# A mixture-of-experts kernel whose first product adds its three half-precision terms in one set of PSUM columns

## Chip, cores and metric

The kernel runs on one core of one Trainium2 chip. The metric is the device time of one execution in microseconds, the median of several runs; lower is better. One further execution was profiled, and the trace, the views and the rows below are from that one.

## What is computed

Three stages follow each other; each one's output is the next one's input:

```python
# 1. a complex linear recurrence with (4, 8, 768, 48) inputs, its output reshaped to x: (3072, 384)
# 2. a mixture of 8 experts, one per token (the argmax of the gate's logits):
for e in range(E):
    mask = e_idx == e
    h = np.maximum(x[mask] @ w1[e], 0.0)              # 384 -> 1024
    out[mask] = gate_w[mask, None] * (h @ w2[e])      # 1024 -> 384
# 3. one dense two-layer network for all tokens, 384 -> 2048 -> 384
h = x @ w_in
g = h * (1.0 / (1.0 + np.exp(-1.702 * h)))
return g @ w_out
```

The change is in stage 2.

## The kernel before

**Halves.** Every float32 operand of the matmuls in stages 2 and 3 is held as two float16 halves, a high one and the remainder, the low one. A product is the sum of three terms: high by high, high by low (of the weights) and low (of the tokens) by high.

**Blocks and quarters.** The tokens are sorted by expert into 26 blocks of 128 tokens; each block has one expert, whose number is read from memory at run time. The 1024 hidden columns are worked in four quarters `q` of 256 (`FQ`). The loop in `moe` runs over the 4 x 26 = 104 pairs `(q, b)`. The weights' tile `w` holds, for each expert and each of the three slices of 128 inputs, 256 high columns and next to them 256 low ones, so a 512-wide operand covers both halves.

**The work for one pair.** `gemm1(q, b)` makes 128 x 256 of `h` in a PSUM tile `ph` (three buffers). `turn(q, b)` transposes it on the tensor engine (PE) into `pt` (two buffers), and writes the two halves of its positive part: the high one, `hT[:, 0]`, by the scalar engine (ACT, L1092), the low one by the vector engine (DVE, L1093), which waits for the high one. `gemm2(q, b)` makes the second product in `py` with six 384-wide matmuls (L1104), and DVE adds it into `acc` (L1109 in the first quarter, L1111 later). `turn` runs two pairs behind `gemm1` and `gemm2` two more behind that (`LAG`), so for each pair PE's order is: `gemm1(b)`, the transposes of `b - 2`, `gemm2(b - 4)`.

**What runs beside it.** All five engines work through their instructions in the order in which the program text issues them. In the first quarter, `split` also transposes each block's tokens (L1067) and makes their halves (L1068 on ACT, L1069 on DVE), and PE reads the block's expert number into a register (`value_load`, L1074). Every matmul whose weights depend on that number has an address computation ahead of it in PE's queue: the program order prints it as `ISA`, the profile as `FUSED_REGOPS`. During each quarter, `halves` makes the next quarter's weights: ACT scales and rounds them (L996, L998, L1001), GpSimd (POOL, L999) or DVE (L1003) takes the remainders. From the second quarter on, `narrow` turns the 64-bit weights of stage 3 into halves in six steps for each tile, with DVE integer operations (L945 to L949, L960, L966), one ACT rounding (L956) and one DVE remainder (L963). The result is stored from a single buffer to memory by the queue of SyncE (SP, L969, `wh<-w`): ACT's next L956 writes that same buffer, so it waits until the store has landed. `narrow` advances by 6 x 21 / 66 = 1.91 steps per pair, that is one tile every 3.14 pairs.

Of the kernel before, what the change touches and what calls it, by code (L numbers as in the profile page):

```python
# [12 lines left out]
F32 = mybir.dt.float32  # L13
# [4 lines left out]
ALU = mybir.AluOpType  # L18
# [4 lines left out]
P = 128  # L23
# [25 lines left out]
FQ = F // NQ  # L49
KD = DM // P  # L50
# [957 lines left out]
def moe(tc, cst, rt, wp, st, we, yd, lo, hi, x, psum, w0=None, w64=None, wh=None, ffn=None):  # L1008


    nc = tc.nc
    with ExitStack() as c2:
# [20 lines left out]
        xT = x.rearrange("p (b h k n) -> p b h k n", b=nb, h=2, k=KD)  # L1033
# [4 lines left out]
        ph_, pt_, py_, ps_ = psum  # L1038
# [32 lines left out]
        def gemm1(q, b):  # L1071
            w = ws[q]
            if b not in reg:
                reg[b] = nc.tensor.value_load(rt.eid[0:1, b:b + 1], min_val=0, max_val=E - 1)  # L1074
            e = reg[b]
            ph = ph_.tile([P, 2 * FQ], F32, tag="ph", name=f"ph{q}_{b}")
            for k in range(KD):
                o = k * 2 * FQ
                nc.tensor.matmul(ph, lhsT=xT[:, b - lo, 0, k, :], rhs=w[:, e, o:o + 2 * FQ], start=k == 0, stop=False)  # L1079
                nc.tensor.matmul(ph[:, :FQ], lhsT=xT[:, b - lo, 1, k, :], rhs=w[:, e, o:o + FQ], start=False, stop=k == KD - 1)  # L1080
            h = wk.tile([P, FQ], F32, tag="h", name=f"h{q}_{b}", bufs=3)
            nc.scalar.copy(h, ph[:, FQ:])  # L1082
            nc.vector.tensor_tensor(out=h, in0=ph[:, :FQ], in1=h, op=ALU.add)  # L1083
            return h

        def turn(q, b, h):
# [62 lines left out]
        for q, b in seq:  # L1149
# [11 lines left out]
            if q == 0 and b > lo:  # L1161
                split(b + 1)
            hs.append((q, b, gemm1(q, b)))
            if q == 0 and b == lo:
                split(b + 1)
# [27 lines left out]
        while hs:  # L1193
            q, b, h = hs.pop(0)
# [475 lines left out]
```

## Time and profile before

| | |
|---|---|
| median of 3 runs | 969.53 us (969.28 to 970.78) |
| the profiled execution's own time | 970.08 us |
| its span, first to last instruction | 968.3 us |
| stage 2's four quarters, from the first second product | 317.45 to 567.3 us of the span |
| mean granted clock of the tensor engine | 0.972 of full speed |

The 1.8 us between the profiled time and its span lie around the program. In the rows below, PE is the tensor engine's matmuls, PEld its weight loads and PEldq its queue's own work (the last is no busy time). A matmul's row gives its duration in the pipeline, which is longer than its distance to the next one; what a matmul costs is read from the starts. The line numbers in the rows are those of the kernel before; in the changed kernel, lines behind L1079 stand one lower in the text, so that the number is one higher (the transposes of `h` are L1090 there, `gemm2` is L1105).

### The profile page before, as it was taken

What the parts mean: (1) busy time and instruction counts of PE and PEld (TensorE: products, weight loads), DVE (VectorE), ACT (ScalarE), POOL (GpSimd) and SP (SyncE); (2) the same over time, 40 slices, a digit from 0 to 9 for tenths busy, and PEclk for the clock granted to TensorE, in tenths of its full rate; (3) what the DMA queues carried; (4) which work ended last, traced back from release to release, by engine and by line L of the source; (5) the groups of instructions that cost most, each with busy time, mean ns of one, the idle gap of its engine ahead of it and who ended that gap; (6) DMA issues with size and microseconds to landing.
All of it is one profiled execution on the core that took longest, in us unless ns stands there. A gap on an engine that the chain in (4) does not pass through costs nothing.

```text
span 968.3 us, 17226 instructions
## 1 busy us (share of the span) xinstructions
PE 892.4 (92%) x5972; PEld 582.7 (60%) x5972; DVE 631.5 (65%) x1376; ACT 536.8 (55%) x1057; POOL 248.0 (26%) x213
## 2 busy tenths in 40 slices
PE   3899899999976999989999999989999999999994
PEld 2778687888865666655556644435645546456662
DVE  4788888888985898988999669996053171340000
ACT  7879768776553876765763456766063261440000
POOL 1212234112434673542530122233120100001110
PEclk9899999999986999999999999999999999999998
DMA  8530432221352664645647331220110000000000
GB/s 277 204 118 31 149 123 84 76 84 43 138 183 62 213 180 135 211 141 171 189 131 239 123 115 56 93 82 11 48 41 9 25 1 17 17 1 32 26 25 19
DMA packets 40403, 94.98 MB, mean 98 GB/s; under 512 B 6546, under 2 KB 19347, under 8 KB 40307
## 3 DMA queue, kind: packets, MB, share of 16 engines
q1 hardware_dynamic: 35138, 77.87, 24.7%
q0 software_dynamic: 4736, 14.69, 5.0%
q8 instruction: 56, 0.92, 0.4%
q10 hardware_dynamic: 432, 1.18, 0.4%
q14 instruction: 41, 0.33, 0.1%
HBM read 74.84 MB, written 18.81 MB: 97 GB/s over the span
## 4 chain that ended last, share of the span: by engine, by line
PE 44%; DVE 14%; DMA 4%; issue 3%; ACT 2%; POOL 0%; ACTq 0%; POOLq 0%; DVEq 0%; SPq 0%
PE fpo L1308 19%; PE fph L1288 12%; PE py L1104 5%; PE ph L1079 4%; DVE w L960 2%; DMA wh<-w 2%; PE ph L1080 2%; DVE acc L1111 2%; DVE x L1292 2%; DVE h L1083 1%; PE pt L1089 1%; DVE hT L1093 1%; DVE w L966 1%; DVE w L963 1%; PE px L1067 1%
## 5 line engine op out<-in xcount | busy, mean ns | idle before, releaser
L1288 PE MATMUL fph<-fx,fw 128*128 128x512 f16 x864 | 192.2, 379 | 5.7 <-DVE x L1292 4.8
L1292 DVE SCALAR_TENSOR_TENSOR x<-fph,x 128x512 f32<-128x512 f32 x96 | 65.9, 688 | 129.8 <-ACT x L1291 128.4
L1288 PEld LDWEIGHTS <-fw 128*128 128x128 f16 x864 | 84.4, 98 | 104.3 <-issue 8.9
L1308 PE MATMUL fpo<-fw,gT 128*128 128x384 f16 x768 | 125.3, 326 | 0.0
L1104 PE MATMUL py<-w,hT 128*128 x624 | 119.0, 328 | 1.1
L1079 PE MATMUL ph<-w,x 128*128 x312 | 108.9, 383 | 1.1 <-ACT x L1068 0.8
L1312 ACT ACTIVATE x<-fpo,fsm 128x384 f32<-128x384 f32 x24 | 13.9, 581 | 167.5 <-PE fpo L1308 167.5
L1308 PEld LDWEIGHTS <-gT 128*128 128x128 f16 x768 | 75.1, 98 | 49.9
L1291 ACT ACTIVATE x<-fph,fsm 128x512 f32<-128x512 f32 x96 | 65.6, 684 | 49.0 <-PE fph L1288 36.1
L999 POOL TENSOR_TENSOR w<-ws,w 128x768 f16<-128x768 f32 x40 | 68.3, 1708 | 85.2 <-ACT w L998 81.5
L1080 PE MATMUL ph<-w,x 128*128 x312 | 85.7, 275 | 1.8 <-DVE x L1069 1.6
L1313 POOL DMA_INDIRECT out<-x,fto x24 | 23.2, 968 | 245.3 <-ACT x L1312 245.3
L1104 PEld LDWEIGHTS <-hT 128*128 128x128 f16 x624 | 61.2, 98 | 32.5 <-issue 4.0
L1082 ACT COPY h<-ph 128x256 f32<-128x256 f32 x104 | 38.5, 370 | 56.2 <-PE ph L1080 49.1
L1308 PE MATMUL fpo<-fw,x 128*128 128x384 f16 x384 | 62.7, 326 | 0.0
L1083 DVE TENSOR_TENSOR h<-ph,h 128x256 f32<-128x256 f32 x104 | 43.4, 417 | 26.5 <-ACT h L1082 24.1
L517 PE MATMUL pt<-c,f 128*96 128x128 f32 x384 | 53.9, 280 | 4.0 <-DVE u L747 1.9
L1308 PEld LDWEIGHTS <-x 128*128 128x128 f16 x384 | 37.6, 98 | 25.0
L517 PEld LDWEIGHTS pt<-c,f 128*96 128x96 f32 x384 | 43.2, 130 | 14.5 <-issue 6.5
L535 PE MATMUL pt<-zq,zk 96*128 96x128 f32 x384 | 51.4, 283 | 0.0
L1079 PEld LDWEIGHTS <-x 128*128 128x128 f16 x312 | 30.8, 99 | 31.3 <-ACT x L1068 1.6
L535 PEld LDWEIGHTS pt<-zq,zk 96*128 96x128 f32 x384 | 47.5, 196 | 2.0 <-ACT zk L525 0.6
(238 smaller groups left out, 1755.7 us busy)
## 6 DMA issues: line engine op xcount, KB each, us to landing
ws<-in_we SPq DMA_DIRECT2D x61, 384.0 KB
w<-in_w SPq DMA_DIRECT2D x32, 384.0 KB
qk<-in_qk SPq DMA_DIRECT2D x6, 1152.0 KB
yd<-acc SPq DMA_DIRECT2D x26, 192.5 KB
xd<-row SPq DMA_DIRECT2D x6, 589.5 KB
ar<-in_ar SPq DMA_DIRECT2D x6, 576.0 KB
ai<-in_ai SPq DMA_DIRECT2D x6, 576.0 KB
v<-in_v SPq DMA_DIRECT2D x6, 576.0 KB
```

The source lines that it names most:

```text
L517: nc.tensor.transpose(pt[:2 * D, h, :], T[FF][:, k, j * H + 4 * i + h].rearrange("p i d -> p (i d)"), cst["ident"])
L535: nc.tensor.matmul(ps[:, h - 4 * i, :], lhsT=T[ZK][:, h, :], rhs=T[ZQ][:, h, :], start=True, stop=True)
L999: nc.gpsimd.tensor_tensor(out=wv[:, :, 1, :], in0=sv, in1=wv[:, :, 0, :], op=ALU.subtract)
L1079: nc.tensor.matmul(ph, lhsT=xT[:, b - lo, 0, k, :], rhs=w[:, e, o:o + 2 * FQ], start=k == 0, stop=False)
L1080: nc.tensor.matmul(ph[:, :FQ], lhsT=xT[:, b - lo, 1, k, :], rhs=w[:, e, o:o + FQ], start=False, stop=k == KD - 1)
L1082: nc.scalar.copy(h, ph[:, FQ:])
L1083: nc.vector.tensor_tensor(out=h, in0=ph[:, :FQ], in1=h, op=ALU.add)
L1104: nc.tensor.matmul(py, lhsT=hT[:, hl, j, :], rhs=w[:, e, o + off:o + off + DM], start=i == 0, stop=i == n - 1)
L1288: nc.tensor.matmul(ph, lhsT=s.wi[f][:, a, k, :], rhs=xT[b][:, k], start=i == 0, stop=i == 3 * KD - 1)
L1291: nc.scalar.activation(h, ph, AF.Sigmoid, scale=sig)
L1292: nc.vector.scalar_tensor_tensor(out=h, in0=ph, scalar=GS, in1=h, op0=ALU.mult, op1=ALU.mult)
L1308: nc.tensor.matmul(po, lhsT=gT[:, f, a, g * P:(g + 1) * P], rhs=s.wo[f][:, b, :], start=i == 0, stop=i == 3 * s.NF - 1)
```

## The change

`gemm1` no longer makes 512 columns per slice, of which the right 256 hold the high-by-low terms. Each of the three terms of a slice is a 256-wide matmul of its own, and all nine add into the same 256 columns of `ph`. ACT then copies the finished sum to `h`, where before it copied the right half and DVE added the left half to it.

```diff
-            ph = ph_.tile([P, 2 * FQ], F32, tag="ph", name=f"ph{q}_{b}")
+            ph = ph_.tile([P, FQ], F32, tag="ph", name=f"ph{q}_{b}")
+            i = 0
             for k in range(KD):
-                o = k * 2 * FQ
-                nc.tensor.matmul(ph, lhsT=xT[:, b - lo, 0, k, :], rhs=w[:, e, o:o + 2 * FQ], start=k == 0, stop=False)
-                nc.tensor.matmul(ph[:, :FQ], lhsT=xT[:, b - lo, 1, k, :], rhs=w[:, e, o:o + FQ], start=False, stop=k == KD - 1)
+                for hx, hw in ((0, 0), (0, 1), (1, 0)):
+                    o = (2 * k + hw) * FQ
+                    nc.tensor.matmul(ph, lhsT=xT[:, b - lo, hx, k, :], rhs=w[:, e, o:o + FQ], start=i == 0, stop=i == 3 * KD - 1)
+                    i += 1
             h = wk.tile([P, FQ], F32, tag="h", name=f"h{q}_{b}", bufs=3)
-            nc.scalar.copy(h, ph[:, FQ:])
-            nc.vector.tensor_tensor(out=h, in0=ph[:, :FQ], in1=h, op=ALU.add)
+            nc.scalar.copy(h, ph)
             return h
```

PE's queue before, the last of the three slices of block 3 in a later quarter and the transposes that follow (`x` is `xT`, `w` the weights, and the first number in a tile's name is the block):

```order
L1079 LDWEIGHTS x
L1079 ISA
L1079 MATMUL ph_3_5678<-w_4482,x 128x512
L1080 LDWEIGHTS x
L1080 ISA
L1080 MATMUL ph_3_5678<-w_4482,x 128x256
L1089 MATMUL pt_1_5688<-c_60,h_1_5626 128x128 x2
```

The same slice in the changed kernel:

```order
L1081 LDWEIGHTS x
L1081 ISA
L1081 MATMUL ph_3_5736<-w_4488,x 128x256
L1081 LDWEIGHTS x
L1081 ISA
L1081 MATMUL ph_3_5736<-w_4488,x 128x256
L1081 LDWEIGHTS x
L1081 ISA
L1081 MATMUL ph_3_5736<-w_4488,x 128x256
L1090 MATMUL pt_1_5748<-c_60,h_1_5683 128x128 x2
```

Two weight loads, two address computations and two matmuls per slice have become three of each; the transposes follow as before.

DVE's queue before, over two pairs of the second quarter:

```order
L1083 TENSOR_TENSOR h_12_5972<-ph_12_5965,h_12_5972 128x256
L1093 SCALAR_TENSOR_TENSOR hT_10_5978<-pt_10_5975,hT_10_5978 128x256
L1111 SCALAR_TENSOR_TENSOR acc_4366<-py_8_5981,rs_4368,acc_4366 128x384
L966 SCALAR_TENSOR_TENSOR w_3_5897<-w_3_5798,w_3_5897 128x384
L1083 TENSOR_TENSOR h_13_6003<-ph_13_5996,h_13_6003 128x256
L1093 SCALAR_TENSOR_TENSOR hT_11_6009<-pt_11_6006,hT_11_6009 128x256
L1111 SCALAR_TENSOR_TENSOR acc_4366<-py_9_6012,rs_4368,acc_4366 128x384
```

The same engine in the changed kernel, from one pair to the next:

```order
L1094 SCALAR_TENSOR_TENSOR hT_11_6089<-pt_11_6086,hT_11_6089 128x256
L1112 SCALAR_TENSOR_TENSOR acc_4366<-py_9_6092,rs_4368,acc_4366 128x384
L945 TENSOR_SCALAR w_4_6102<-w_4_5967 128x384
L946 TENSOR_SCALAR w_4_6102<-w_4_6102 128x384
L949 TENSOR_SCALAR w_4_6102<-w_4_6102 128x384
L1094 SCALAR_TENSOR_TENSOR hT_12_6126<-pt_12_6123,hT_12_6126 128x256
```

The addition (L1083) that stood ahead of each L1093 is gone, and a pair's work on DVE begins with the low half of `hT`; nothing else changes places.

## Rows read from the trace of the kernel before

**Rows 1.** Engines: busy us (share of the span), instructions; the page's first part.

```profile
PE 892.4 (92%) x5972; PEld 582.7 (60%) x5972; DVE 631.5 (65%) x1376; ACT 536.8 (55%) x1057; POOL 248.0 (26%) x213
```

**Rows 2.** Busy us (instructions) by engine, PEclk, DMA, GB/s; first products' quarters, core 0.

```profile
317.45:383.40 65.95, 64.28 (x426) 43.37 (x425) 59.11 (x147) 48.41 (x143) 34.78 (x45) 1.00 0.57 177
383.40:446.00 62.60, 58.70 (x366) 35.87 (x365) 56.43 (x124) 41.24 (x88) 27.39 (x16) 1.00 0.50 161
446.00:511.50 65.50, 60.58 (x366) 36.33 (x365) 59.43 (x129) 44.14 (x95) 27.75 (x16) 0.97 0.55 170
511.50:567.30 55.80, 55.62 (x357) 35.29 (x356) 42.67 (x102) 22.64 (x63) 4.09 (x5) 1.00 0.51 164
```

**Rows 3.** The page's group: busy us, mean ns, idle before, releaser.

```profile
L1083 DVE TENSOR_TENSOR h<-ph,h 128x256 f32<-128x256 f32 x104 | 43.4, 417 | 26.5 <-ACT h L1082 24.1
```

**Rows 4.** In order of time, 420.7 to 423.05: start us, us, engine, line, operation.

```profile
420.80 0.38 PE L1079 MATMUL ph<-w,x 128*128 x1
...
421.02 0.27 PE L1080 MATMUL ph<-w,x 128*128 x1
421.02 0.10 PEld L1079 LDWEIGHTS <-x 128*128 128x128 f16 x1
...
421.12 0.38 PE L1079 MATMUL ph<-w,x 128*128 x1
...
421.77 0.38 PE L1089 MATMUL pt<-c,h 128*128 128x128 f32 x2
...
422.04 1.14 PE L1104 MATMUL py<-w,hT 128*128 x6
...
423.01 0.38 PE L1079 MATMUL ph<-w,x 128*128 x1
```

**Rows 5.** In order of time, PE, 328.5 to 329.0, first quarter.

```profile
328.58 0.49 PE L1067 MATMUL px<-c,r 128*128 128x128 f32 x3
328.91 0.38 PE L1079 MATMUL ph<-w,x 128*128 x1
```

**Rows 6.** PE's queue, L1104, 430.84 to 431.39: count, min/median/max ns, first and last start.

```profile
L1104 PEldq FUSED_REGOPS  x5: 55/55/55, 430.8 to 431.4; - x5
```

**Rows 7.** PE's queue, L1074, 328.24 to 330.60, same columns.

```profile
L1074 PEldq FUSED_REGOPS  x2: 151/151/151, 328.2 to 330.6; - x2
L1074 PEldq TENSOR_LOAD <-eid x1: 298/298/298, 330.2 to 330.2; - x1
```

**Rows 8.** Who waited for whom, 383.4 to 511.5: us, times, longest us.

```profile
ACT w L956 <- DMA wh<-w: 15.1, 9, 2.9
DVE h L1083 <- ACT h L1082: 11.0, 12, 3.7
```

**Rows 9.** The chain that ended last by line, 383.4 to 511.5.

```profile
by line: DMA wh<-w 15.7%; DVE acc L1111 12.1%; DVE w L960 11.9%; DVE h L1083 8.6%; DVE hT L1093 7.7%; issue 6.3%; DVE w L963 5.9%; PE py L1104 5.5%; DVE w L966 3.7%; PE ph L1079 3.5%; ACT ws L996 3.5%; DMA ws<-in_we 3.0%; ACT w L998 2.9%; A
```

**Rows 10.** The same chain by line, 317.45 to 383.4.

```profile
by line: PE py L1104 35.9%; PE ph L1079 23.7%; PE ph L1080 12.6%; PE px L1067 8.4%; PE pt L1089 7.9%; DVE rs L1056 2.2%; issue 1.7%; DVE x L1069 1.6%; ACT w L1001 1.1%; ACT h L1082 1.0%; DVE acc L1109 0.8%; ACT x L1068 0.7%; DVE h L1083 0.6
```

**Rows 11.** In order of time, 393.0 to 396.8: a copy, its addition, a store.

```profile
393.16 0.35 ACT L1082 COPY h<-ph 128x256 f32<-128x256 f32 x1
...
394.68 0.42 DVE L1083 TENSOR_TENSOR h<-ph,h 128x256 f32<-128x256 f32 x1
...
396.72 0.39 SPq L969 DMA_DIRECT2D wh<-w  x1
```

**Rows 12.** In order of time, 400.9 to 403.0: after that store.

```profile
401.00 0.52 ACT L956 ACTIVATE w<-w 128x384 f16<-128x384 f32 x1 [2.88 <-DMA wh<-w]
...
402.15 0.36 ACT L1082 COPY h<-ph 128x256 f32<-128x256 f32 x1
...
402.41 0.39 ACT L1092 ACTIVATE hT<-pt 128x256 f16<-128x256 f32 x1
402.55 0.42 DVE L1083 TENSOR_TENSOR h<-ph,h 128x256 f32<-128x256 f32 x1 [1.22 <-ACT h L1082]
...
402.89 0.41 DVE L1093 SCALAR_TENSOR_TENSOR hT<-pt,hT 128x256 f16<-128x256 f32 x1
```

## Prediction

> **What bounds the kernel now.** I read the page first: PE is busy for 92% of the span and DVE for 65% [rows 1]. Such averages say little about one stage, so next came the busy time by stretch, cut at the starts of the four quarters [rows 2]. There the reader should see DVE: 56.43 of 62.60 us in the second quarter and 59.43 of 65.50 us in the third, next to a PE that looks busy as well. Third came the order of time, which gives what PE needs when nothing holds it up. Six first-product matmuls take 0.97 us (420.80 to 421.77), two transposes 0.27 us at most and 0.22 us at the pace of a 256-wide matmul, six second-product matmuls 0.97 us (422.04 to 423.01) [rows 4]. That is 2.17 us for a pair (q, b). In the first quarter three more transposes add 0.33 us (328.58 to 328.91) [rows 5]: 2.50 us.
>
> Against these floors the stretches show what is lost. PE runs 60 more instructions in the first stretch than in the second [rows 2], three for each of 20 pairs, so its floor is 20 x 2.50 + 6 x 2.17 = 63.0 of 65.95 us: 2.9 us lost. The second quarter's is 26 x 2.17 = 56.4 of 62.60 (6.2 lost), the third's 56.4 of 65.50 (9.1 lost). The fourth is at its floor for nearly all its length.
>
> Where do those 15.3 us go? In the chain for 383.4 to 511.5, PE's lines are small and DVE's large: L1083, the addition that the change removes, has 8.6% of 128.1 us, 11.0 us [rows 9]. In the first quarter the same line has 0.6%, and PE nearly everything [rows 10]. The waits say how the two engines catch each other: ACT waits 15.1 us in all for the store `wh<-w` to land [rows 8]. One case in order of time: the copy of 393.16 is done at 393.51, but the addition begins only at 394.68, because DVE is behind; the store behind it is issued at 396.72 [rows 11]; ACT, which needs the store's buffer, stands until 401.00 [rows 12], and with it the copies and the halves that PE needs.
>
> **The change, part by part.**
>
> *Columns.* A pair's first product has 3 x (512 + 256) = 2304 columns before and 9 x 256 = 2304 after. The pace of one 512-wide and one 256-wide matmul is 0.32 us (420.80 to 421.12) [rows 4]; three 256-wide ones at the 0.10 to 0.11 us between L1080 and the next L1079 are 0.32 us as well. What is left is a few nanoseconds for each of three more instructions, at most 0.01 us a pair; I take 0.0075 us x 104 = **+0.8 us**.
>
> *Weight loads.* 312 more, 0.10 us each. The load that starts at 421.02 runs under the 256-wide matmul of 421.02, and the next matmul starts on time at 421.12 [rows 4], so 0.10 us of load fits under 256 columns: nothing, with about 0.01 us of cover to spare. The Trainium skill ("TensorE: Matmul & The Clock Gate", "What overlaps and what doesn't") states that a load overlaps a running matmul only where the two use different row groups; these use all rows. By that rule the sum would be about 31 us worse (below), and the rows above speak against it.
>
> *Address computations.* Also 312 more, and here PE's queue has a pace of its own. Five of L1104 start between 430.84 and 431.39, from 430.8 to 431.4 [rows 6]: four distances in 0.50 to 0.55 us, about 0.134 us each. That is faster than the six second-product matmuls they serve (0.97 / 6 = 0.162 us [rows 4]), so it is not the array that sets it, and slower than a 256-wide matmul (0.107 us). The queue runs ahead of the array, so what counts is the sum for a pair. In the first quarter one round, from one L1074 to the next, takes 2.30 to 2.36 us [rows 7] for twelve such matmuls and the reading of the expert's number; it fits under 2.50 us. With three more it is 2.35 + 3 x 0.134 = 2.75 us and no longer fits. Twenty pairs at 2.75 are 55.0 us, where 20 x 2.50 + 2.9 = 52.9 us are spent now: +2.1 if the slower pace swallows all that is lost there today, +5.0 if it swallows nothing. I take **+3.7**, a little above the middle, since the lost time has other causes (DVE's L1056 and L1069 stand in that chain [rows 10]). In the other quarters 15 x 0.134 = 2.01 us stays under 2.17: between 0 and, if the queue needs 0.03 us a pair more than PE, 78 x 0.03 = +2.3; I take **+0.4**, for pairs just after a stall, when the queue has no lead.
>
> *The addition.* 104 x 417 ns = 43.4 us of DVE's busy time go [rows 3]. What it holds up is less, 0.34 us (402.55 to 402.89 [rows 12]), so 11.0 us in the chain are 32 passes. In 12 cases DVE had been waiting for the copy [rows 8]. Then little is won: the next operation, L1093, also needs ACT's L1092, which starts at 402.41 and takes 0.39 us, so it could start at about 402.82 in place of 402.89 [rows 12]: 0.07 us, times 12, 0.8. The other 20 passes give 0.34 each, 6.8. I take **-7.4** of 7.6, since PE's floor is near. Bounds: -1, if every gap closes with another wait; -11.0, the whole of the line in the chain.
>
> *The waits.* The transposes now need ACT's copy, which is earlier than the addition was; their other wait, for the buffer `pt` that L1093 frees two pairs before, stays and is the later of the two. A buffer `ph` comes free after the copy. Nothing else is queued differently. At the drain behind the last pair one addition lies open: **-0.3**.
>
> *Sum.* 0.8 + 3.7 + 0.4 - 7.4 - 0.3 = -2.8: 967.3 us against the profiled execution's 970.08, which is 0.55 above the median; so 966.7 in terms of the median.
>
> **The rivals.**
>
> *The queue wins.* The first quarter pays in full (+5.0), the others 1 to 2, and the gain in the middle shrinks to 2 to 4, because ACT, the store and DVE close into a loop without the addition: store at 396.72, buffer free at 401.00, L1093 at 402.89 [rows 11, 12] is 6.2 us, and with L1111 and L960 behind it easily more than the 3.14 x 2.17 = 6.8 us of a tile. For it: the store's latency is the chain's first entry with 15.7%, L960's 11.9% is larger than the addition's [rows 9]. Against it: 20 of 32 passes were not released by ACT. Sum +2 to +5, 971.5 to 974.5. It decides once the gain in the middle is under 4.9 us. Chance 0.24.
>
> *Both cancel.* Within 0.2%, about what a measurement of this kernel can tell from no change (1.9 us): gain in the middle of 3 to 6.7. Near 969.5. Chance 0.18.
>
> *DVE was the root.* DVE's lag is what makes stores late, so without it most of the 15.3 us go, 11 to 13, and the first quarter pays only 2.1: 960 to 962. For it: DVE has 90% in those quarters [rows 2] and would have about 75%. Against: L960's duration and the store remain. Chance 0.1.
>
> *The queue is no limit.* The address rows last 55 ns each [rows 6]; if only that counted, fifteen take 0.83 us, the terms 3.7 and 0.4 fall away, and the sum is -6.9: 962.6. Against it stands the distance of 0.134 us, which holds a matmul, its load and its address together. The Trainium skill (same page, "Wait — 56ns, not 53.3ns?") gives the queue about 62 ns for each matmul where the sequencer decodes it, and with such a figure too it would be no limit; it says nothing of computed addresses. Chance 0.06.
>
> *The loads don't hide.* 312 x 0.10 = +31, 1000 us; [rows 4] speak against it. Chance 0.02.
>
> **How the numbers follow.** The forecast (a gain over 1.9 us, up to 9) has 0.40, its own range 961.5 to 967.6. Faster is this with the third and the fourth rival, 0.56; same 0.18; slower 0.26. The range 960.5 to 973.5 leaves out the loads, the far end of the first rival and part of the third.
>
> **What would show it.** Right: nine matmuls 0.11 us apart in the second to fourth quarters and a pair at 2.17 to 2.20; a first quarter whose pairs lie about 2.75 us apart with PE's idle time put to no engine; the second and third quarters shorter by some 7 us, with ACT's wait for `wh<-w` well under 15.1. Wrong: a first quarter that keeps 2.50 us (the queue hides it), pairs at 2.25 or more in the fourth quarter (it is dearer than I think), or L956 still waiting 15 us (the loop lives without the addition).

## The result

The changed kernel takes 977.39 us in the median of 5 runs (974.60 to 979.78), the kernel before 969.85 (969.28 to 970.78, 5 runs): a ratio of 1.0084, 95% interval 1.0066 to 1.0101. The change costs about 8 us. The forecast, 966.7, had the sign wrong, and the time lies above the stated range, which ended at 973.5.

The profiled execution took 979.78 us with a span of 977.9, 9.6 more than before. These rows of its page answer to [rows 1] and [rows 3]: the engines, the granted clock in the 40 slices, and the group of the nine first-product matmuls.

```profile
PE 906.2 (93%) x6284; PEld 617.4 (63%) x6284; DVE 605.4 (62%) x1272; ACT 537.8 (55%) x1057; POOL 248.1 (25%) x213
...
PEclk9889999899986999999999999999999999999998
...
L1081 PE MATMUL ph<-w,x 128*128 x936 | 128.0, 273 | 1.8 <-ACT x L1068 0.8
```

DVE is busy for 605.4 us against 631.5. That is 26.1 us less, while the additions' rows had 43.4 [rows 3]. PE has 312 matmuls more. All 936 matmuls of the first product are now one group, and its line doesn't tell what an address computation costs.

The next question is where the time lies. The cuts are the first token transpose (`px`, L1067) and the first second product of the second, the third and the fourth quarter. Windows of the changed kernel, columns as in [rows 2]: the first blocks with the first quarter; the second quarter; the third; everything behind.

```profile
308.31:391.71 83.40, 81.53 (x571) 59.11 (x572) 56.70 (x135) 54.38 (x163) 42.80 (x59) 0.97 0.55 164
391.71:455.20 63.49, 59.95 (x444) 43.34 (x443) 52.62 (x99) 41.42 (x88) 27.87 (x16) 1.00 0.54 166
455.20:519.99 64.79, 60.40 (x444) 43.23 (x443) 53.78 (x102) 44.14 (x95) 27.20 (x16) 1.00 0.54 165
519.99:977.91 457.92, 437.62 (x2493) 244.89 (x2491) 198.20 (x382) 174.78 (x345) 66.66 (x69) 0.99 0.16 51
```

The same for the kernel before; its second and third quarters are in [rows 2], 62.60 and 65.50.

```profile
305.41:383.39 77.98, 74.86 (x478) 49.97 (x479) 65.56 (x165) 53.74 (x163) 43.50 (x59) 0.97 0.57 174
511.47:968.26 456.79, 436.58 (x2430) 238.90 (x2428) 205.16 (x405) 175.16 (x345) 66.77 (x69) 0.99 0.16 51
```

The first blocks and the first quarter went from 77.98 to 83.40 (+5.4). The second and the third quarters went from 128.1 to 128.3 (+0.2), though DVE is busy for 52.62 of 63.49 us in the second and no longer for 56.43 of 62.60. What lies behind grew from 456.79 to 457.92 (+1.1). That is 6.7 of the 9.6 us; the other 2.9 lie ahead of 308.31 us, where both kernels run the same instructions. Over the thirteen profiles of this study the first `px` starts anywhere between 302.3 and 309.0 us, and it comes the later the lower the tensor engine's mean granted clock is up to there: 0.95 of full speed in the two profiles that reach it by 302.4 us, 0.93 and 0.92 in the two that need over 308. So these 2.9 us are put down to the clock and not to the change, and a profile is read here by stretches and not by its end.

**The first quarter.** One pair of the changed kernel there, PE in order of time (start, duration in the pipeline, line, count):

```profile
339.52 0.49 PE L1067 MATMUL px<-c,r 128*128 128x128 f32 x3
339.97 1.36 PE L1081 MATMUL ph<-w,x 128*128 x9
341.17 0.38 PE L1090 MATMUL pt<-c,h 128*128 128x128 f32 x2
341.38 1.14 PE L1105 MATMUL py<-w,hT 128*128 x6
342.36 0.49 PE L1067 MATMUL px<-c,r 128*128 128x128 f32 x3
```

The nine first-product matmuls take from 339.97 to 341.17, 1.20 us or 0.133 us each, and the next pair begins 2.84 us after this one. PE's queue, L1074's rows in 339.5 to 342.4 (count, min/median/max ns, first and last start), shows the round from one expert number to the next:

```profile
L1074 PEldq FUSED_REGOPS  x2: 151/151/151, 339.6 to 342.3; - x2
```

The round is 2.7 us, 339.6 to 342.3, where it was 2.4, 328.2 to 330.6 [rows 7]. For comparison, a pair in the second quarter, same columns as above:

```profile
403.65 1.15 PE L1081 MATMUL ph<-w,x 128*128 x9
404.64 0.38 PE L1090 MATMUL pt<-c,h 128*128 128x128 f32 x2
404.86 1.14 PE L1105 MATMUL py<-w,hT 128*128 x6
405.84 0.38 PE L1081 MATMUL ph<-w,x 128*128 x2
```

The same nine matmuls take 0.99 us (403.65 to 404.64), 0.11 each, and the pair 2.19 (403.65 to 405.84). So the narrow matmuls and their loads are not slow in themselves. They are slow where the queue has no lead.

The blocks ahead of the first second product belong to this stretch too. Here they are in the kernel before, in the changed one, and in e8, a kernel that has before's instructions in this stretch:

```profile
305.41:317.45 12.04, 10.59 (x54) 6.61 (x55) 6.46 (x19) 5.34 (x20) 8.72 (x15) 0.78 0.57 158
308.31:321.34 13.03, 11.47 (x69) 8.10 (x70) 5.22 (x15) 5.47 (x20) 9.25 (x15) 0.81 0.59 167
305.31:316.58 11.27, 10.03 (x54) 6.31 (x55) 6.45 (x19) 5.34 (x20) 8.72 (x15) 0.85 0.58 169
```

The change pays 1.0 us here, at no lower a granted clock. But the clock alone makes 0.8 us as well: e8 needs 11.27 us at 0.85 where before needs 12.04 at 0.78. Part of these blocks runs at the lower of the clock's two levels, 1.2 GHz, in every profile. In the rest of the first quarter the clock is at 2.4 GHz throughout. That rest took 65.95 us before [rows 2] and takes 70.37 now (83.40 less 13.03).

Note how badly the busy time shows this: PE counts as busy for 81.53 of 83.40 us in this stretch, and the chain that ended last, by line for 321.3 to 391.7, holds PE and next to nothing else:

```profile
by line: PE ph L1081 44.9%; PE py L1105 36.0%; PE px L1067 9.3%; PE pt L1090 8.1%; ACT w L998 1.2%; issue 0.5%; ACT ws L996 0.2%; ACTq L998 0.0%
```

A first-product matmul's row lasts 0.27 us in the mean (the group above) and covers the distance to the next one whether that is 0.11 or 0.133. Only the starts tell.

**The middle.** Who waited for whom in 391.7 to 520, the second and third quarters of the changed kernel (us, times, longest us):

```profile
DVE hT L1094 <- ACT hT L1093: 18.6, 17, 3.8
ACT w L956 <- DMA wh<-w: 17.3, 9, 3.9
...
PE pt L1090 <- DVE hT L1094: 6.6, 10, 1.3
```

And the chain for the same time, by line:

```profile
by line: DMA wh<-w 19.4%; DVE w L960 10.4%; PE py L1105 8.6%; DVE acc L1112 8.6%; PE ph L1081 8.5%; issue 7.3%; DVE w L963 5.6%; DVE hT L1094 5.6%; ACT ws L996 5.0%; ACT w L998 4.3%; ACT h L1084 3.1%; ACT hT L1093 3.0%; DMA ws<-in_we 2.9%; 
```

Against [rows 8] and [rows 9]: ACT still waits for the store, 17.3 us in 9 times where it was 15.1 in 9, and the store's share of the chain rose from 15.7% to 19.4%. DVE's 11.0 us of waiting for the copy became 18.6 us of waiting for ACT's high half. The 11.0 us of L1083 are gone from the chain, and the stretch is no shorter.

DVE's own busy time fell by less than the additions' rows. In the middle it went from 115.9 us [rows 2] to 106.4, 9.4 less, though 52 rows of 0.42 us left. Neighbouring rows of DVE overlap a little, which is one part of that. The other is that the rows of `narrow` got longer, L966's for example (before, then the changed kernel, second and third quarters):

```profile
L966 DVE SCALAR_TENSOR_TENSOR w<-w,w 128x384 int32<-128x384 int32 x16 | 11.6, 724 | 0.0
L966 DVE SCALAR_TENSOR_TENSOR w<-w,w 128x384 int32<-128x384 int32 x16 | 15.0, 940 | 0.0
```

In order of time, a long one of the changed kernel:

```profile
405.19 1.73 POOL L999 TENSOR_TENSOR w<-ws,w 128x768 f16<-128x768 f32 x1 [0.19 <-ACT w L998]
405.34 2.00 DVE L966 SCALAR_TENSOR_TENSOR w<-w,w 128x384 int32<-128x384 int32 x1
```

The shortest rows of L966 last 0.55 us; this one begins beside POOL's L999 and ends 0.42 us after it. Counted over the middle, 29 rows of DVE in either kernel last more than 0.06 us longer than the shortest of their line. All are `narrow`'s, and every one lies beside a row of L999. In sum they are 14.5 us longer than that before and 21.1 in the changed kernel. No run moves L999, so it is not shown that POOL makes them long, nor what that costs.

### The profile page after: what moved, and what is told of

Read it like the earlier page. It is cut to its first block, busy times and chain, and to the rows that moved or that the text cites. A ratio compares the mean times of both kernels' runs of the same rounds, so it can differ in the third digit from the quotient of the medians.

```text
span 977.9 us, 18038 instructions
## 1 busy us (share of the span) xinstructions
PE 906.2 (93%) x6284; PEld 617.4 (63%) x6284; DVE 605.4 (62%) x1272; ACT 537.8 (55%) x1057; POOL 248.1 (25%) x213
## 3 DMA queue, kind: packets, MB, share of 16 engines
q1 hardware_dynamic: 35138, 77.87, 24.6%
## 4 chain that ended last, share of the span: by engine, by line
PE 45%; DVE 12%; DMA 4%; ACT 3%; issue 3%; POOL 0%; ACTq 0%; SPq 0%; POOLq 0%; DVEq 0%
PE fpo L1309 18%; PE fph L1289 12%; PE ph L1081 7%; PE py L1105 6%; DMA wh<-w 3%; DVE w L960 2%; DVE x L1293 2%; DVE acc L1112 1%; PE pt L1090 1%; DVE hT L1094 1%; PE px L1067 1%; DVE gT L1298 1%; DVE w L963 1%; DVE w L966 1%; DMA fr<-yd,sidx 1%
## 5 line engine op out<-in xcount | busy, mean ns | idle before, releaser
L1081 PE MATMUL ph<-w,x 128*128 x936 | 128.0, 273 | 1.8 <-ACT x L1068 0.8
L1081 PEld LDWEIGHTS <-x 128*128 128x128 f16 x936 | 91.2, 98 | 30.4 <-ACT x L1068 1.4
L999 POOL TENSOR_TENSOR w<-ws,w 128x768 f16<-128x768 f32 x40 | 68.2, 1706 | 90.8 <-ACT w L998 90.8
L1094 DVE SCALAR_TENSOR_TENSOR hT<-pt,hT 128x256 f16<-128x256 f32 x104 | 43.7, 421 | 51.0 <-ACT hT L1093 49.9
L517 PE MATMUL pt<-c,f 128*96 128x128 f32 x384 | 54.9, 284 | 3.2 <-DVE f L491 3.2
L1309 PEld LDWEIGHTS <-x 128*128 128x128 f16 x384 | 37.6, 98 | 25.0
L1112 DVE SCALAR_TENSOR_TENSOR acc<-py,rs,acc 128x384 f32<-128x384 f32 x78 | 47.6, 610 | 1.4 <-PE py L1105 0.8
```

Of the source, the lines that this page charges most:

```text
L517: nc.tensor.transpose(pt[:2 * D, h, :], T[FF][:, k, j * H + 4 * i + h].rearrange("p i d -> p (i d)"), cst["ident"])
L999: nc.gpsimd.tensor_tensor(out=wv[:, :, 1, :], in0=sv, in1=wv[:, :, 0, :], op=ALU.subtract)
L1081: nc.tensor.matmul(ph, lhsT=xT[:, b - lo, hx, k, :], rhs=w[:, e, o:o + FQ], start=i == 0, stop=i == 3 * KD - 1)
L1094: nc.vector.scalar_tensor_tensor(out=hT[:, 1], in0=pv, scalar=0.0, in1=hT[:, 0], op0=ALU.max, op1=ALU.subtract)
L1112: nc.vector.scalar_tensor_tensor(out=a, in0=py, scalar=s, in1=a, op0=ALU.mult, op1=ALU.add)
L1309: nc.tensor.matmul(po, lhsT=gT[:, f, a, g * P:(g + 1) * P], rhs=s.wo[f][:, b, :], start=i == 0, stop=i == 3 * s.NF - 1)
```

## Experiments

Two things were to be told apart. In the first quarter: is it the number of computed addresses, or the number of matmuls and loads, or their width? In the middle: why did the addition's time not come back; because something else needs the slot, because of the single store buffer, or because DVE never was the limit? The table gives all runs; "first" is from the first `px` to the second quarter, "middle" the second and third quarters, "rest" what lies behind, each in us of the profiled execution. Ratios are against the kernel before on the same chip.

| run | ratio (95%) | first | middle | rest |
|---|---|---|---|---|
| before | 1 | 77.98 | 128.1 | 456.8 |
| the change | 1.0084 (1.0066 to 1.0101) | 83.40 | 128.3 | 457.9 |
| e13, the change again | 1.0068 (1.0050 to 1.0087) | 83.77 | 127.4 | 458.3 |
| e1, before without the addition | 0.9958 (0.9941 to 0.9976) | 76.33 | 125.9 | 456.7 |
| e2, change with a DVE pass | 1.0085 (1.0052 to 1.0119) | 83.49 | 131.0 | 456.9 |
| e3, change, two store buffers | 1.0011 (0.9985 to 1.0036) | 83.53 | 122.5 | 457.1 |
| e4, before, two store buffers | 1.0021 (1.0004 to 1.0037) | 77.87 | 130.0 | 456.8 |
| e5, change, no computed address in `gemm1` | 0.9980 (0.9961 to 0.9998) | 75.82 | 128.7 | 456.5 |
| e6, change from the second quarter on | 0.9989 (0.9972 to 1.0006) | 77.85 | 126.0 | 458.1 |
| e7, e6 with two store buffers | 0.9947 (0.9931 to 0.9963) | 78.07 | 122.8 | 459.2 |
| e8, before, three `hT` buffers | 1.0004 (0.9990 to 1.0018) | 77.09 | 128.8 | 456.3 |
| e9, change, six computed addresses | 0.9994 (0.9979 to 1.0009) | 76.75 | 128.1 | 456.0 |
| e12, e1 with two store buffers | 0.9917 (0.9893 to 0.9941) | 77.02 | 121.8 | 455.7 |

**e1: the addition alone.** The old matmuls stay; only DVE's pass goes, and with it the term of high tokens by low weights, which is left out of `h`.

```diff
-            nc.scalar.copy(h, ph[:, FQ:])
-            nc.vector.tensor_tensor(out=h, in0=ph[:, :FQ], in1=h, op=ALU.add)
+            nc.scalar.copy(h, ph[:, :FQ])
```

> The kernel before, with its 512-wide and 256-wide matmuls, but without the addition on DVE: ACT copies the left 256 columns, so the term of high tokens by low weights is left out of h. Theory A (the store's buffer holds up the second and third quarters, the addition only looks as if it did): the two stay at 124 to 128.5 us together (before: 62.6 + 65.5 = 128.1), the first at 64 to 66, the whole at 967 to 970.5. Rival B (the addition did hold them up, and the longer PE queue of the change eats the gain): the two fall to about 120, the whole to 961 to 964.

Windows: first blocks with the first quarter, second quarter, third quarter.

```profile
302.40:378.73 76.33, 74.09 (x478) 49.82 (x479) 56.28 (x135) 53.69 (x163) 43.58 (x59) 0.98 0.58 178
378.73:440.56 61.83, 58.61 (x366) 35.86 (x365) 51.85 (x99) 41.27 (x88) 27.25 (x16) 1.00 0.54 170
440.56:504.67 64.11, 59.69 (x366) 35.62 (x365) 53.75 (x102) 43.96 (x95) 27.41 (x16) 1.00 0.53 167
```

Without the addition the whole is 0.42% shorter, 4.1 us. Of these the middle gives 2.1 (61.83 + 64.11 against 128.1) and the first stretch 1.6. Some 0.7 of the 1.6 are the clock's in the first blocks (0.85 as in e8): e12, which has the same instructions there and 0.80, gains 1.0 (77.02). So DVE's pass has a price, but not the 7.4 us of the forecast, although 104 passes left DVE here as well. The whole came out below the 967 to 970.5 us that were expected.

**e2: the change with the pass put back.** DVE reads `ph` and `h` once more and writes their maximum, which changes no value.

```diff
             nc.scalar.copy(h, ph)
+            nc.vector.tensor_tensor(out=h, in0=ph, in1=h, op=ALU.max)
```

> The changed kernel with a DVE pass of the old size put back behind the copy: h = max(ph, h), which changes no value. DVE has its old load, PE its new one. Theory A: the second and third quarters stay within 3 us of the change's 128.3, the first at 70 to 71, the whole within 3 us of the change's 977.4. Rival B: the two quarters grow by 5 or more, the whole to 983 or more.

Same windows.

```profile
302.25:385.74 83.49, 81.47 (x571) 58.98 (x572) 66.49 (x165) 54.26 (x163) 44.04 (x59) 0.98 0.55 164
385.74:450.61 64.87, 60.34 (x444) 43.25 (x443) 58.46 (x124) 41.27 (x88) 27.65 (x16) 1.00 0.51 154
450.61:516.78 66.17, 60.78 (x444) 44.07 (x443) 58.92 (x129) 44.19 (x95) 27.82 (x16) 0.97 0.55 169
```

The first stretch is as long as the change's, 83.49 against 83.40 and 83.77: its length does not hang on DVE. The middle is 2.8 to 3.7 us longer than in the two profiles of the change, but the medians do not show it (976.93 against 977.39 and 976.21). Up to 2 us of it may be the clock's: this profile's third quarter has a mean of 0.97, the change's has 1.00, and 0.03 of 66 us is 2 us (an estimate for a stretch that PE limits throughout, which this one is not). In the changed kernel, then, the missing pass is worth between nothing and some 3 us.

**e3: the change with two buffers for the store.** The space comes from the fourth `hT` buffer.

```diff
-                dst = o[i] = pool.tile([P, 2, DM], F16, tag="w16", name=f"w16_{m}", bufs=1)
+                dst = o[i] = pool.tile([P, 2, DM], F16, tag="w16", name=f"w16_{m}", bufs=2)
-            hT = wk.tile([P, 2, FQ // P, P], F16, tag="hT", name=f"hT{q}_{b}", bufs=4)
+            hT = wk.tile([P, 2, FQ // P, P], F16, tag="hT", name=f"hT{q}_{b}", bufs=3)
```

> The changed kernel with two buffers for the stored halves (w16) instead of one; to make room, hT has three buffers instead of four. Theory A: ACT's L956 no longer waits for the store, the second and third quarters lose under 6 us instead of 14.9 (119 us together or less), the whole about 968 to 971. Rival B: the store was no cause; L956's wait goes, but the quarters stay above 125 and the whole at 975 or more.

Same windows, and below them two of the waits in 392.5 to 515.1.

```profile
308.99:392.52 83.53, 81.44 (x571) 59.04 (x572) 56.39 (x135) 54.26 (x163) 43.38 (x59) 0.97 0.55 164
392.52:451.84 59.32, 58.19 (x444) 43.63 (x443) 54.31 (x99) 41.25 (x88) 27.98 (x16) 1.00 0.57 178
451.84:515.06 63.22, 60.64 (x444) 43.19 (x443) 57.25 (x102) 44.24 (x95) 27.10 (x16) 1.00 0.54 168
```

```profile
ACT ws L996 <- DMA ws<-in_we: 11.3, 8, 4.1
...
ACT w L956 <- DVE w L966: 7.3, 7, 1.8
```

The middle fell from 128.3 to 122.5 us, where 119 or less was expected, and the wait for the store is gone from the list. ACT's L956 now waits 7.3 us for DVE, and ACT's L996 waits 11.3 us for the weights that the next quarter needs. The second quarter is at 59.32 us, where PE's floor is 56.4; the third still loses 6.8.

**e4: the same edit on the kernel before.**

> The kernel before, addition and all, with two buffers for the stored halves (w16) and three instead of four for hT. Theory A (the single store buffer is what holds up the second and third quarters): ACT's wait for the store goes, the two quarters fall from 128.1 to 120 to 123 us as they did for the changed kernel, the whole to 963 to 966. Rival: with the addition in place DVE takes the store's place as what holds them up; the quarters stay above 126, the whole within 2 us of before.

Windows of the second and third quarters, and the wait of L956 in 383.3 to 513.3.

```profile
383.32:447.28 63.96, 59.40 (x366) 35.74 (x365) 61.75 (x124) 41.58 (x88) 27.66 (x16) 1.00 0.50 159
447.28:513.30 66.02, 60.04 (x367) 35.64 (x365) 62.24 (x129) 44.61 (x95) 27.27 (x16) 1.00 0.52 168
```

```profile
ACT w L956 <- DVE w L966: 10.9, 8, 2.7
```

Nothing is won; the middle is 130.0 us. DVE is busy for 61.75 of 63.96 and 62.24 of 66.02 us, 97% and 94%. The store no longer holds ACT up, but now ACT's L956 waits 10.9 us for DVE's L966: by these rows DVE itself is the limit. Its 253 rows take 124.0 us here where the same number took 115.9 before [rows 2]; why they are longer no run shows. With e1, e3 and e12 this makes a square.

| middle, us | one store buffer | two store buffers |
|---|---|---|
| with the addition | 128.1 | 130.0 |
| without it, old matmuls | 125.9 | 121.8 |
| without it, the change | 128.3, 127.4 | 122.5 |

**e8: the control for the `hT` buffers.** Before, with three `hT` buffers and one for the store.

> The kernel before with three instead of four buffers for hT and nothing else, the control for the room that two store buffers took. If three are enough: second and third quarters at 127 to 130 us together, the whole within 2 us of before, and the missing gain of two store buffers with the addition in place is real. Rival: the third buffer is missed, the two quarters grow by 4 or more and the whole by 4, so that it hid a gain there.

Ratio 1.0004 (0.9990 to 1.0018), middle 128.8 us, and ACT waits 20.1 us for the store. The missing fourth `hT` buffer costs nothing that could be told, so what e3, e4 and e12 show is put down to the store's second buffer.

**e12: neither the addition nor the single buffer.** The edits of e1 and of e3 together, on the kernel before.

> The kernel before without the addition (ACT copies the left 256 columns; the term of high tokens by low weights is left out) and with two store buffers. If addition and store buffer each hide the other: second and third quarters at 120 to 123 us together, first at 64 to 66, the whole at 960 to 963.5, that is 2 to 5 below the same without the second buffer. Rival (the gain of the two buffers came from the narrow matmuls' slower first quarter): 125 or more, the whole at 965.

```profile
381.30:440.33 59.03, 58.14 (x367) 35.95 (x365) 54.56 (x99) 41.20 (x88) 27.63 (x16) 1.00 0.56 179
440.33:503.07 62.74, 60.04 (x366) 35.63 (x365) 57.39 (x102) 44.34 (x95) 27.12 (x16) 1.00 0.54 171
```

59.03 and 62.74 us: the middle is 6.3 us shorter than before. The whole is 0.83% shorter, 8.0 us, where the addition alone gave 4.1 and the buffers alone lost 2.0. The two limits hide each other: whichever is taken away alone, the other keeps most of the stretch. The medians agree: if the two did not act on each other, the ratio would be 0.9958 x 1.0021 = 0.9979, well outside the interval of 0.9917 (0.9893 to 0.9941).

**e5: no computed address in the first product.** Nine narrow matmuls and nine loads stay, but the weights are picked by a number that is known when the program is built, so they are not always those that the routing asks for.

```diff
-    rhs=w[:, e, o:o + FQ]
+    rhs=w[:, b * E // MAXB, o:o + FQ]
```

> The changed kernel with a fixed expert for each block in the first product alone, so that its nine matmuls have no address computation (the first product takes other weights than the routing asks for). Theory Q (PE's queue is the bound of the first quarter): the first quarter's pairs fall from 2.80 to 2.50 us and the quarter from 70.4 to 63 to 66 us; the whole 4 to 7 us below the change, 970 to 973. Rival (something else, such as the weight loads or PSUM, makes the narrow matmuls slow): pairs stay at 2.7 or more, the whole within 2 us of the change.

Window of the first blocks and the first quarter.

```profile
304.57:380.39 75.82, 73.90 (x571) 58.07 (x572) 55.76 (x134) 53.81 (x163) 43.50 (x59) 0.98 0.60 180
```

It has the change's 571 matmuls and 572 loads in this stretch (as the first of the change's windows), and takes 75.82 us in place of 83.40. Some 0.8 of these 7.6 us are the clock's in the first blocks (0.85 here as in e8); the rest of the quarter, all of it at full clock, takes 64.60 us in place of 70.37, and 64.97 in e1, which has the old matmuls. The whole falls under the kernel before, below the 970 to 973 us that were expected. So the extra matmuls and loads cost nothing here; the computed addresses cost what the clock does not explain.

**e9: six computed addresses, as before.** Nearest to a single edit: nine matmuls, of which only the low-by-high term takes its weights by a fixed number (so not always the right ones).

```diff
-    rhs=w[:, e, o:o + FQ]
+    rhs=w[:, b * E // MAXB if hx else e, o:o + FQ]
```

> The changed kernel with a fixed expert in the third of each three matmuls (low tokens by high weights) alone: nine narrow matmuls and nine loads as in the change, but six address computations, as many as before (the low tokens meet other weights than the routing asks for). Theory Q (what counts is the number of address computations): the first quarter at 64 to 66.5 us with pairs at 2.50, the whole 966 to 969, near the fixed expert's 967.2. Rival (the number of matmuls or loads counts too): pairs at 2.6 or more, the whole at 971 or more.

```profile
303.88:380.63 76.75, 74.47 (x571) 58.81 (x572) 56.34 (x135) 53.83 (x163) 43.75 (x59) 0.97 0.59 178
```

76.75 us, 6.7 under the change, and a ratio of 0.9994. The pairs of its first quarter lie 2.50 us apart in the median, those of the change 2.80. The three computed addresses that the change adds to each pair are what it loses by: the medians differ by 8.9 and 7.7 us (968.49 against 977.39 and 976.21), and 6.7 to 7.0 of that lie in the first stretch.

**e6: the change from the second quarter on.** `gemm1` keeps its old form where `q` is 0 and takes the new one otherwise.

```diff
+            if q:
+                ph = ph_.tile([P, FQ], F32, tag="ph", name=f"ph{q}_{b}")
...
+                        nc.tensor.matmul(ph, lhsT=xT[:, b - lo, hx, k, :], rhs=w[:, e, o:o + FQ], start=i == 0, stop=i == 3 * KD - 1)
...
+                nc.scalar.copy(h, ph)
+                return h
```

> The first quarter as before (512-wide and 256-wide matmuls, addition on DVE), the later ones as changed. Theory Q (the loss is the queue's, in the first quarter and its first blocks): the first quarter is back at 65 to 66 us, the stretch ahead of it too, and 5 to 7 of the change's 7.5 us are gone: 970 to 972. Rival (the narrow matmuls cost as much in the other three quarters): 974 or more.

```profile
304.15:382.00 77.85, 74.71 (x493) 51.45 (x494) 64.63 (x161) 53.72 (x163) 43.59 (x59) 0.97 0.58 175
```

The first stretch is back at 77.85 us and the whole is the kernel before's within what can be told (0.9989, 0.9972 to 1.0006), 968.1 us where 970 to 972 was expected. What is left of the change, the narrow form in three quarters, has a middle of 126.0 us and loses about 1.3 of that gain behind it (458.1).

**e7: e6 with two store buffers.** The edits of e6 and e3 together; nothing is left out of the result.

> The kernel of e6 with two store buffers and three of hT. If the two causes are separate, their gains add: first quarter 65 to 66, second and third 120 to 123 together, the whole 962 to 966, about what e4 has. If the queue costs something in the later quarters also when nothing stalls, it stays 2 us or more above e4.

Windows: first blocks with the first quarter, second quarter, third quarter.

```profile
305.07:383.14 78.07, 75.05 (x493) 51.44 (x494) 64.77 (x161) 53.77 (x163) 43.54 (x59) 0.96 0.57 174
383.14:442.17 59.03, 58.54 (x444) 43.51 (x443) 54.32 (x99) 41.23 (x88) 27.55 (x16) 1.00 0.57 176
442.17:505.91 63.74, 60.39 (x444) 43.19 (x443) 56.98 (x102) 44.33 (x95) 26.86 (x16) 1.00 0.55 170
```

964.48 us, ratio 0.9947 (0.9931 to 0.9963): faster than both kernels by 0.5% and more, and than the old form with two buffers (e4, 1.0021). The narrow form is worth having, after all, where the queue has time for it and where DVE's free time is not taken back by the store.

**e13: the change again**, unedited.

> The changed kernel once more, beside the others. The stretch from the first token transpose to the second quarter at 83 to 84 us (78.0 before), second and third quarters 126 to 130, the rest within 2 us of before's 456.7; what the first stage (whose instructions are the same) adds differs from execution to execution. The whole at 975 to 978.

976.21 us, ratio 1.0068 (1.0050 to 1.0087), and stretches of 83.77, 127.4 and 458.3. The split of the loss repeats: +5.8, -0.7 and +1.5.

## Why the prediction was wrong

*Columns* (+0.8) and *Weight loads* (0): right as far as the runs go. Nine 256-wide matmuls with their nine loads took 0.99 us against 0.97 for the six before [rows 4], 0.02 a pair where at most 0.01 was said. e5 and e9 carry them all and are no slower than the kernel before. The Trainium skill ("TensorE: Matmul & The Clock Gate", "What overlaps and what doesn't") lets a load overlap a running matmul only if the row groups differ. By that rule nine loads on all rows, at 0.10 us each [rows 4], would have added 0.9 us to a pair; they added nothing, and the measurement decides against the rule for these loads.

*Address computations*: the mechanism was right, and the terms too small. "In the first quarter" the forecast had +3.7, with +5.0 as the worst. Measured is +5.4 and +5.8 from the first `px` on, and 6.7 to 7.0 when the change is compared with e9, which has lost the addition as well; most of the difference is what the missing addition gives there (e12: -1.0). Two things were missed. The pairs came at 2.80 us in the median, 2.84 in the pair shown, and not at 2.75: twenty times 0.30 us are 6.0, not 5.0. And the pairs ahead of the first second product pay too: from the first `px` to it 13.03 us pass against 12.04, +1.0, which no term held. The allowance for lost time that a slower pace would swallow (1.3 of the 5.0 us) was too large: behind the first blocks the change is 5.4 and 5.8 us slower than e9 (64.95 us there), nearly the whole 6.0. In the other quarters the forecast was +0.4. The stretch behind the third quarter says +1.1 and +1.5; over all kernels it is 456.9 to 459.2 with nine computed addresses there and 455.7 to 456.8 with six or none. The queue's pace explains little of it: the fourth quarter's pairs lie 2.18 us apart in the median, 2.17 before. From its first to its last second product that quarter took 54.9 us before and takes 57.0 in the change's profile, and the 2.1 us sit in two long pairs near its end (2.92 and 3.46 us). In the second of them PE stands idle ahead of stage 3's first matmuls:

```profile
559.58 0.35 PE L1240 MATMUL fps<-fsm,ones 128*128 128x1 f32 x2 [0.67 <-DVE fsm L1236]
```

In the middle an effect of the number of addresses cannot be told from the spread: without the addition and with one buffer, the kernels with nine lie at 126.0 to 128.3, those with fewer at 125.9 to 128.7. The rival *The queue is no limit* is refuted by the 0.133 us for a matmul with a load and a computed address, and by the loss going away when three of the nine computed addresses are fixed (e9). The Trainium skill ("TensorE: Matmul & The Clock Gate", "Wait — 56ns, not 53.3ns?") gives about 62 ns for each matmul that the sequencer decodes. Whether that figure holds for a matmul without a computed address no run here shows; with one the queue took 0.133 us.

*The addition* (-7.4) is the step that failed: "The other 20 passes give 0.34 each, 6.8." It makes the larger part of the miss: of the 10.7 us between forecast and median some 7 lie in the middle, some 2 in the first stretch and 1 behind. In the changed kernel the middle came out at +0.2 and -0.7 us in two profiles, in e9 at 0.0, and alone (e1) the same removal gave 2.1 there and 4.1 in all. The share of a line in the chain says how much of the end's history went through it. It does not say how much sooner the end comes without it, because a second limit lay right behind: the single store buffer, with L956, L963 (which write what is stored) and the store in a ring. The chain did name it, with 15.7%, larger than the addition's 8.6% [rows 9]. The forecast took that for a consequence of DVE's lag; it is a limit of its own. Each of the two edits alone gives -2.1 and +1.9 in the middle, both give -6.3. So 6.3 of the foreseen 7.4 were there to be had, and needed a second buffer. The forecast also took each pass's 0.34 us as won, while part of DVE's freed time went into longer rows of `narrow` beside POOL's L999 (21.1 us in sum where it was 14.5); what that costs the whole no run isolates.

*The waits* (-0.3): not seen apart from the rest.

*The rivals.* *The queue wins* told the mechanism, down to the loop without the addition, and gave 971.5 to 974.5; it was 3 to 6 us short, since the gain in the middle was nought and not 2 to 4 and the first blocks were not in it. *DVE was the root* is refuted by e1. Of the signs named ahead, three came as foreseen: matmuls 0.11 us apart in the later quarters with a pair at 2.19, a first quarter at the queue's pace, and the one for being wrong, L956 still waiting over 15 us. One sign was ill chosen: the first quarter's loss does not show as PE's idle time, since the matmuls' rows cover it.

What stays open: why PE stands ahead of stage 3's first matmuls in some profiles of the narrow form (0.67 us in the change's, 1.17 in e13's) and not in others (e2, e3), what makes the middle of the one-buffer kernels without the addition lie anywhere from 125.9 to 128.7 us, and why e2's longer middle does not show in its median. The clock may have a part in the last two: the mean granted clock is 1.00 in nearly all of the second and third quarters, but 0.97 in e5's second, in e2's third and in before's third [rows 2]. In e3, e7 and e12 the third quarter still loses over 6 us; ACT's 11 us of waiting for the weights' loads (e3) stands there, and so do DVE's long rows beside L999. Neither was tried.

## What to carry over

Splitting a matmul into narrower ones is free for the array only while the queue keeps pace: compare, for each stage, the sum of the queue's work (here 0.133 us for each matmul with a computed address, and the reading of the register) with the sum of the array's, and take the larger. The share of a line in the chain that ended last is not what its removal gives (here 11.0 us of share, and 0 to 2 us gained in that stretch); look for the next ring that closes without it (here a buffer of one, held until a store lands), and cost the pair of edits together. A form that pays in one quarter may cost in another of the same loop, so it can be chosen by quarter.

## What the runs showed of the hardware

PE's queue sends matmuls with a load and a computed address at 0.133 us apart (339.97 to 341.17 for nine), close to the 0.134 that stood at 384 columns where the queue was faster than the array [rows 6]; at 256 columns the array needs 0.11, so the queue sets the pace as soon as its lead is gone. The first stage of the program, with the same instructions in all thirteen profiles, took between 302.3 us, at a mean granted clock of 0.95, and 309.0 us, at 0.92. That is nearly as much as the whole effect of the change, and the reason why every reading here was made by stretches. Rows of DVE that work beside a row of POOL's L999 can be up to 1.5 us longer than the shortest of their line (2.00 us against 0.55 for L966); all 29 clearly longer rows of the middle, before and after the change, are of this kind.
